# Fused attention and two expert layers on one core: the two halves of a null-key mean on two partitions

## The chip, the cores and the metric

The kernel runs on one core of a Trainium2 chip. The metric is device time in microseconds (us), the median of several runs of the whole program. A core has five engines with instruction streams of their own: PE (TensorE, matrix multiplication), DVE (VectorE), ACT (ScalarE), POOL (GpSimd) and SP (SyncE, which here only issues DMAs). "PEld" is PE's loading of the stationary operand, which the profile lists apart from the matmuls. "SPq" and "ACTq" are the instructions by which SP and ACT issue DMAs.

## The reference

Three layers run one after the other. The part that the change touches is the first, an attention in which a query sees only the keys that fall into the same hash bucket:

```
q_bucket, k_bucket = 6 sign bits of q @ proj and of k @ proj, as a number
mask   = q_bucket[:, None] == k_bucket[None, :]
scores = where(mask, q @ k.T / 8, -1e9)
attn   = softmax(scores)
x      = attn @ v            # 2 batches, 8 heads, 768 tokens, 64 columns
x      = gated rational layer: g(x @ w_in) @ w_out         # 512 -> 2048 -> 512
out    = top-1 of 8 experts: gate * relu(x @ w1[e]) @ w2[e]  # 512 -> 1024 -> 512
```

A query whose bucket holds no key gets -1e9 everywhere, so its softmax is uniform and its result is the mean of all rows of v. That is the "null-key" term.

## The kernel before, in words

The attention works in 24 units: 2 batches, 3 thirds of the queries (256 each), 4 pairs of heads. For each unit `prep` turns q and k around on PE, splits them into a high and a low float16 part and computes the bucket bits (`ee`, `eq`). `stack_a` and `stack_b` let SP copy these pieces by DMA into operands of 128 partitions (`qa`, `qb`, `kp`). `pass1` (matmul L638, maximum L644) finds the largest score of each query. `pass2` computes the scores again (L718, L719), takes the exponential on ACT (L723 for the first batch, L728 and L729 for the second) and sums the weighted rows of v (L687) into one PSUM tile `av` of 4 blocks of 128 queries, 65 columns each: 64 of v and one of ones, which collects the sum of the weights. In the first batch these matmuls are float32, in the second float16 in three terms.

The null-key term goes into the same tile. `flags` (L612 on) turns a row of query maxima around on PE (L617, tile `pm`), DVE makes a 0/1 flag of each (`mf`), and SP copies the flags by DMA into one partition of the tile `FL` (partition 0 for even units, 32 for odd ones). `values` computes, once for each pair of heads and batch (8 times in all), the mean of v by a matmul with ones (L416), which ACT scales into `v32`. DVE stores its float16 rounding (L419, L438) and the rounding error (L420, L439) as two slots of the tile `vmr`, whose last column holds 1 in the first slot and 0 in the second. With the last block of keys of a unit, each of the 4 query blocks gets two more matmuls (the loop ahead of L687): stationary operand one row of 128 flags, moving operand one row of `vmr`, 65 columns. One adds the high part, the other the low part.

Beside the attention run the splitting of the second layer's weights (tiles `raw`, `bits`, `win`, `wo`) and, from unit 7 on, that layer itself for the query blocks that are ready (matmuls L783 and L824, activation chain L797 to L810). After the attention come the last block of the second layer and then the expert layer (L1291 to L1396).

The order of the instructions on each engine is settled when the program is built. Unit 0 (`start`) and all that follows the second layer are written out by hand. Between them a scheduler places the instructions by priorities and its own estimate of times. An edit in one place can therefore move instructions elsewhere. On each engine the order is then fixed: an instruction that waits holds up those behind it.

Of the kernel before, what the change touches and what calls it, by code (L numbers as in the profile page):

```python
# [8 lines left out]
F16 = mybir.dt.float16  # L9
# [3 lines left out]
ALU = mybir.AluOpType  # L13
# [4 lines left out]
P = 128  # L18
B, H, S, D = 2, 8, 768, 64
NPAIR = H // 2  # L20
# [31 lines left out]
NV = 34  # L52
# [68 lines left out]
def tile_kernel(  # L121
# [16 lines left out]
    dve, act, pool, pe, sp = nc.vector, nc.scalar, nc.gpsimd, nc.tensor, nc.sync  # L138
# [10 lines left out]
    def ps_hid(i, nm):  # L149
        return ps_h.tile([P, 512], F32, tag=f"h{i % 2}", name=nm)  # L150
# [137 lines left out]
    anchor = {}  # L288

    def ps_misc(nm, dtype=F32):  # L290
        if phase["b"]:
            return ps_sc.tile([P, 512], dtype, tag="sc", name=nm)
        phase["n"] += 1
        if phase["n"] % 3 == 0:
            return ps_h.tile([P, 512], dtype, tag="h1", name=nm)
        return ps_x.tile([P, 512], dtype, tag="x", name=nm)
# [79 lines left out]
    def prep(ap, a1p, u):  # L376
# [29 lines left out]
        progress["ready"] = u  # L406
        yield

    def values(ap, u):
        va, vmr = VAS[u % NPAIR], VMR[u % NPAIR]  # L410
        if units[u][0] == 0:
            yield
            pv = ps_misc(f"pv{u}")
            pv3 = pv[:, : 2 * D].rearrange("p (h c) -> p h c", h=2)
            for j in range(NT):
                pe.matmul(pv3[0:NV], ones32, VFS[u][:, :, j, 0:D], start=(j == 0), stop=(j == NT - 1))  # L416
            v32 = ap.tile([NV, 2, D], F32, tag="v32", name=f"v32{u}", bufs=1)
            act.activation(v32, pv3[0:NV], AF.Copy, scale=1.0 / S)
            dve.tensor_copy(vmr[:, 0, :, 0:D], v32)  # L419
            dve.tensor_tensor(vmr[:, 1, :, 0:D], v32, vmr[:, 0, :, 0:D], op=ALU.subtract)  # L420
            yield
            return
        vr = raws["v", u]
        pool.memset(va[:, :, :, D : D + 1], 1.0)
        if u in VAC:
            act.copy(va[:, :, :, 0:D], vr)
        else:
            dve.tensor_copy(va[:, :, :, 0:D], vr)
        (dve if u in VLD else pool).tensor_tensor(va[:, :, :, D + 1 :], vr, va[:, :, :, 0:D], op=ALU.subtract)
        yield  # L430
        pv = ps_misc(f"pv{u}")
        pv3 = pv[:, : 2 * (2 * D + 1)].rearrange("p (h c) -> p h c", h=2)
        for j in range(NT):
            pe.matmul(pv3, ones16, va[:, :, j, :], start=(j == 0), stop=(j == NT - 1))
        v32 = ap.tile([NV, 2, D], F32, tag="v32", name=f"v32{u}", bufs=1)
        act.activation(v32, pv3[0:NV, :, D + 1 :], AF.Copy, scale=1.0 / S)
        dve.scalar_tensor_tensor(v32, pv3[0:NV, :, 0:D], 1.0 / S, v32, op0=ALU.mult, op1=ALU.add)
        dve.tensor_copy(vmr[:, 0, :, 0:D], v32)  # L438
        dve.tensor_tensor(vmr[:, 1, :, 0:D], v32, vmr[:, 0, :, 0:D], op=ALU.subtract)  # L439
        yield  # L440

    def clear_k(eng, t):
# [171 lines left out]
    def flags(ap, u, m16, c0, c1, both=True):  # L614
        n, cs = c1 - c0, slice(c0 * P, c1 * P)
        pm = ps_misc(f"pm{u}_{c0}", F16)
        pe.transpose(pm[0:n, :P], m16[:, :n], ident16)  # L617
        mf = ap.tile([NC, 2, P], F16, tag="mf", name=f"mf{u}_{c0}", bufs=1)
        if both:
            dve.tensor_copy(mf[0:n, 0, :], pm[0:n, :P])  # L620
        dve.tensor_single_scalar(out=mf[0:n, 1, :], in_=pm[0:n, :P], scalar=-MFLOOR, op=ALU.is_ge)
        if both:
            row = QBS[u % 2][96:97, 1, :, :].rearrange("p h q -> p (h q)")
            sp.dma_start(row[:, cs], mf[0:n, 0, :])
        f0 = 32 * (u % 2)
        anchor["fl"] = sp.dma_start(FL[f0 : f0 + 1, cs], mf[0:n, 1, :])


    def pass1(ap, u):
# [26 lines left out]
    def pass2(ap, u, later):  # L656
        b, th, hp = units[u]
        qb = QBS[u % 2]
        va, vmr = VAS[hp], VMR[hp]
        f0 = 32 * (u % 2)  # L660
        st = {}

        def weigh(hhs, j, eh, el):
            if "av" not in st:
                if phase["b"] == 0 and u % 2 == 1:
                    st["av"] = ps_hid(0, f"av{u}")
                else:
                    st["av"] = ps_av.tile([P, 512], F32, tag="av", name=f"av{u}")
            av3 = st["av"][:, : NC * (D + 1)].rearrange("p (c d) -> p c d", c=NC)
            for n in range(len(hhs) * TH):  # L670
                hh, c = hhs[n // TH], hhs[0] * TH + n
                ts_ = slice(n * P, (n + 1) * P)
                if el is None:
                    mms = [((0, D + 1), eh[:, ts_], VFS[hp][:, hh, j, :])]
                else:
                    mms = [
                        ((0, D + 1), eh[:, ts_], va[:, hh, j, 0 : D + 1]),
                        ((0, D), eh[:, ts_], va[:, hh, j, D + 1 :]),
                        ((0, D + 1), el[:, ts_], va[:, hh, j, 0 : D + 1]),
                    ]  # L680
                if j == NT - 1:
                    for i in range(2):
                        lr = FL[f0 : f0 + 1, c * P : (c + 1) * P], vmr[f0 : f0 + 1, i, hh, :]
                        mms.insert(0, ((0, D + 1), *lr))
                for i, (o, l, r) in enumerate(mms):
                    first = "first" not in st
                    m = pe.matmul(  # L687
                        av3[:, c, o[0] : o[1]], l, r,
                        start=first, stop=(j == NT - 1 and i == len(mms) - 1), skip_group_check=True,
                    )  # L690
                    if first:
                        st["first"] = m
                    elif j == 0:
                        order_after(m, st["first"])
            if j == NT - 1 and hhs[-1] == 1:
                with tc.high_priority(offset=FOFF):
                    finish(av3)
# [303 lines left out]
    with ExitStack() as actx:  # L1001
        ap = actx.enter_context(tc.tile_pool(name="ap", bufs=2, side="right"))
        a1p = actx.enter_context(tc.tile_pool(name="a1p", bufs=1, side="right"))
# [19 lines left out]
            t.rearrange("p h t c -> p (h t c)").bitcast(F16)[:, :NVA].rearrange("p (h t c) -> p h t c", h=2, t=NT)  # L1023
            for t in VFS
        ]
        VMR = [a1p.tile([NV, 2, 2, D + 1], F16, name=f"vmr{i}") for i in range(NPAIR)]
        FL = a1p.tile([NV, NC * P], F16, name="FL")
        clear_k(dve, KPS[0])
        clear_q(dve, 0)
        for t in VMR:  # L1030
            pool.memset(t[:, 0, :, D : D + 1], 1.0)
            pool.memset(t[:, 1, :, D : D + 1], 0.0)

        def weights():
            ahead = list(wq)
# [21 lines left out]
        for u in range(NU):  # L1057
            assert u == 0 or progress["s1"] >= u * N1, u
            for st, _ in enumerate(pass2(ap, u, later) if u else p2, 0 if u else 1):
# [27 lines left out]
                n = min(goal - progress["s1"], N1P) if u > 0 else N1 - progress["s1"] - (NT - 1 - st) if progress["ready"] else 0  # L1087
# [185 lines left out]
    halves = [s for s in range(NEARLY, NMAIN) if half(s)]  # L1273
# [245 lines left out]
    with tc.manual_schedule(engines=EALL):  # L1519
# [26 lines left out]
        for t in range(TH):  # L1546
# [15 lines left out]
            op=ALU.mult,  # L1562
# [26 lines left out]
            op=ALU.is_equal,  # L1589
# [7 lines left out]
            op=ALU.is_equal,  # L1597
# [98 lines left out]
```

## Time and profile before

| | |
|---|---|
| median of 3 runs | 806.24 us (805.02 to 807.43) |
| profiled execution | 808.09 us, of which its span is 806.4 us |
| PE busy in the span | 737.3 us, 91% |
| DVE busy | 629.4 us, 78% |
| ACT busy | 552.3 us, 68% |
| POOL busy | 321.8 us, 40% |
| mean granted clock of PE | 0.965 of full |

The span runs from the first to the last instruction of one execution. Busy time is not bound time: an engine that is busy 78% of the span may be what everyone waits for in one stretch and idle in another, so the tables by stretch further down are what counts. The granted clock is the share of PE's full clock that the chip allowed.

### The profile page before, as it was taken

The page shows a single profiled execution, that of the slowest core. Times are in us where ns is not written, and L with a number is a line of the kernel's source. Part 1 is how long each engine was busy: PE and PEld are TensorE (multiplying, and loading weights), DVE is VectorE, ACT ScalarE, POOL GpSimd, SP SyncE. Part 2 cuts the span into 40 slices and gives each one's busy share as a digit, 9 for nine tenths or more (in the row PEclk, how much of TensorE's full clock was granted, in tenths as well). Part 3 has the DMA queues.
Part 4 walks back from the last instruction along what each step waited for, and adds up shares of the span by engine and source line. Part 5 has one row for each costly group of instructions (what it writes and reads, how often), then busy time and mean ns, then how long its engine had stood idle before and what let it go on. Part 6 is the DMA issues. An engine that isn't in the chain of part 4 may idle for free. (4 is left out here: it accounts for less than half of the span.)

```text
span 806.4 us, 19020 instructions
## 1 busy us (share of the span) xinstructions
PE 737.3 (91%) x6951; PEld 523.9 (65%) x6951; DVE 629.4 (78%) x1214; ACT 552.3 (68%) x953; POOL 321.8 (40%) x291
## 2 busy tenths in 40 slices
PE   3869799999999999999999999999578999999995
PEld 1448578877777667776777777667345676666763
DVE  5577888789996787768666856776877898989981
ACT  2325335557666777787888887884875698988981
POOL 5101120335353555555565564441520374334320
PEclk9789999989999999999999999999699999999998
DMA  9556554325542211111111100000601358765950
GB/s 220 118 126 178 151 140 137 99 78 141 141 119 46 75 25 22 28 42 24 28 21 35 22 2 18 11 1 28 235 1 40 100 210 280 255 206 188 350 191 3
DMA packets 76297, 83.36 MB, mean 103 GB/s; under 512 B 38634, under 2 KB 56582, under 8 KB 76200
## 3 DMA queue, kind: packets, MB, share of 16 engines
q1 hardware_dynamic: 43672, 50.88, 21.3%
q10 hardware_dynamic: 30064, 24.27, 10.9%
q0 software_dynamic: 2464, 6.95, 2.4%
q8 instruction: 56, 0.92, 0.5%
q14 instruction: 41, 0.34, 0.1%
HBM read 113.92 MB, written 6.95 MB: 150 GB/s over the span
## 5 line engine op out<-in xcount | busy, mean ns | idle before, releaser
L687 PE MATMUL av<-vf,ehl 128*128 128x65 f32 (+2 forms) x1440 | 136.7, 227 | 0.7 <-ACT ehl L723 0.5
L801 POOL TENSOR_TENSOR w<-w,qq 128x512 f32<-128x512 f32 x48 | 61.4, 1279 | 162.6 <-ACT w L798 151.1
L1346 DVE SCALAR_TENSOR_TENSOR wl<-wr,wh 128x1024 f16<-128x1024 f32 x88 | 104.1, 1231 | 9.1 <-ACT wh L1338 9.1
L644 DVE TENSOR_REDUCE mx<-s 128x1 f32<-128x512 f32 (+1 forms) x138 | 93.8, 684 | 19.7 <-PE s L638 17.8
L783 PEld LDWEIGHTS <-winh 128*128 128x128 f16 x768 | 74.8, 98 | 24.0 <-issue 1.4
L1338 ACT ACTIVATE wh<-wr 128x1024 f16<-128x1024 f32 x88 | 87.6, 1056 | 0.0
L730 POOL TENSOR_TENSOR ehl<-e,ehl 128x512 f16<-128x512 f32 x60 | 69.4, 1160 | 37.6 <-ACT ehl L729 33.5
L824 PE MATMUL px<-woh,gh 128*128 128x512 f16 x192 | 74.6, 388 | 9.1 <-ACT gh L809 9.1
L1366 PE MATMUL ph<-xst,wh 128*128 128x128 f16 (+1 forms) x1088 | 80.9, 212 | 1.7 <-ACT xst L1293 1.7
L687 PEld LDWEIGHTS av<-vf,ehl 128*128 128x128 f32 x576 | 77.0, 197 | 5.5 <-ACT ehl L723 1.0
L1366 PE MATMUL ph<-xst,wl 128*128 128x128 f16 (+1 forms) x544 | 79.8, 212 | 0.0
L1366 PEld LDWEIGHTS <-wh 128*128 128x128 f16 x1088 | 73.9, 98 | 7.8 <-issue 5.0
L1396 POOL DMA_INDIRECT out_dram<-y,sidx x15 | 38.0, 2533 | 97.8 <-ACT y L1395 97.8
L718 PE MATMUL s<-qb,kp 128*128 128x256 f16 x288 | 73.6, 278 | 3.5 <-DVE mx L644 2.6
L824 PE MATMUL px<-woh,gl 128*128 128x512 f16 x192 | 73.2, 388 | 1.7 <-DVE gl L810 1.7
L824 PE MATMUL px<-wol,gh 128*128 128x512 f16 x192 | 74.6, 389 | 0.0
L719 PE MATMUL s<-qb,kp 128*128 128x256 f16 x288 | 71.3, 279 | 0.0
L723 ACT ACTIVATE ehl<-s 128x512 f32<-128x512 f32 (+1 forms) x78 | 42.8, 572 | 34.2 <-PE s L719 32.5
L805 POOL TENSOR_TENSOR w<-w,h 128x512 f32<-128x512 f32 x48 | 64.1, 1335 | 3.7
L638 PE MATMUL s<-kp,qa 128*128 128x512 f16 (+1 forms) x184 | 52.9, 339 | 9.6 <-DMA kp<-ee 5.1
L783 PE MATMUL ph<-xth,winh 128*128 128x256 f16 x384 | 58.9, 274 | 0.5 <-DVE gl L810 0.5
L783 PE MATMUL ph<-xtl,winh 128*128 128x256 f16 x384 | 59.0, 274 | 0.0
(318 smaller groups left out, 1809.1 us busy)
## 6 DMA issues: line engine op xcount, KB each, us to landing
wr<-in_moe_w_dram SPq DMA_DIRECT2D x88, 512.0 KB
woh<-in_moe_w_dram SPq DMA_DIRECT2D x36, 512.0 KB
wol<-in_moe_w_dram SPq DMA_DIRECT2D x36, 512.0 KB
rawi<-in_moe_w_in_dram ACTq DMA_DIRECT2D x16, 512.0 KB
rawo<-in_moe_w_out_dram ACTq DMA_DIRECT2D x16, 512.0 KB
x2d<-x SPq DMA_DIRECT2D x12, 256.0 KB
qb<-hq SPq DMA_DIRECT2D x47, 64.0 KB
kp<-hk SPq DMA_DIRECT2D x15, 192.0 KB
```

The source lines that it names most:

```text
L644: anchor["max"] = dve.reduce_max(flat[:, i : i + len(parts)], ps.rearrange("p (n k) -> p n k", n=len(parts)), axis=AX)
L687: m = pe.matmul(av3[:, c, o[0] : o[1]], l, r, start=first, stop=(j == NT - 1 and i == len(mms) - 1), skip_group_check=True,)
L718: pe.matmul(o, kp[:, 1, ks], qb[:, 0, hh, :], start=True, stop=False)
L719: anchor["s2"] = pe.matmul(o, kp[:, 0, ks], qb[:, 1, hh, :], start=False, stop=True)
L730: (dve if j in ELD else pool).tensor_tensor(el, e32, eh, op=ALU.subtract)
L783: pe.matmul(ph[:, i * QC : (i + 1) * QC], w[:, dc, fs], x[:, dc, :], start=(m == 0 and dc == 0), stop=(m == 2 and dc == NDC - 1),)
L801: pool.tensor_tensor(w, w, qq, op=ALU.mult)
L805: pool.tensor_tensor(w, w, h32, op=ALU.add)
L824: pe.matmul(pxs[t], g[:, ts_], w[:, f, :], start=(f == 0 and n == 0), stop=(f == NFC - 1 and n == 2))
L1338: act.activation(WH[s, c], raw(s, c), AF.Copy, scale=sc_of(c))
L1346: dve.scalar_tensor_tensor(WL[s, c], raw(s, c), sc_of(c), WH[s, c], op0=ALU.mult, op1=ALU.subtract)
L1366: pe.matmul(ph[:, f4, :w], m[s, c][:, fs], x, start=(n == 0), stop=(n == 3 * NDC - 1))
```

## The change

The high and the low half of the mean no longer stand in two slots of one partition but on two neighbouring partitions: high on partition 0 (and 32), low on all others, among them 1 (and 33). The flags are copied twice, to both partitions. One matmul with two rows then adds both halves. A new function `halves` fills the tile: DVE rounds `v32` into a tile `v16` and writes the rounding error to all 34 partitions of `vmr`, then POOL copies the rounded row over it on partitions 0 and 32.

```diff
+    def halves(ap, u, v32):
+        vmr = VMR[u % NPAIR]
+        v16 = ap.tile([NV, 2, D], F16, tag="v16", name=f"v16{u}", bufs=1)
+        dve.tensor_copy(v16, v32)
+        dve.tensor_tensor(vmr[:, :, 0:D], v32, v16, op=ALU.subtract)
+        for r in (0, 32):
+            pool.tensor_copy(vmr[r : r + 1, :, 0:D], v16[r : r + 1])
...
     def values(ap, u):
...
-            dve.tensor_copy(vmr[:, 0, :, 0:D], v32)
-            dve.tensor_tensor(vmr[:, 1, :, 0:D], v32, vmr[:, 0, :, 0:D], op=ALU.subtract)
+            halves(ap, u, v32)
...
     def flags(ap, u, m16, c0, c1, both=True):
...
-        anchor["fl"] = sp.dma_start(FL[f0 : f0 + 1, cs], mf[0:n, 1, :])
+        for r in (f0, f0 + 1):
+            anchor["fl"] = sp.dma_start(FL[r : r + 1, cs], mf[0:n, 1, :])
...
     def pass2(ap, u, later):
...
                 if j == NT - 1:
-                    for i in range(2):
-                        lr = FL[f0 : f0 + 1, c * P : (c + 1) * P], vmr[f0 : f0 + 1, i, hh, :]
-                        mms.insert(0, ((0, D + 1), *lr))
+                    mms.insert(0, ((0, D + 1), FL[f0 : f0 + 2, c * P : (c + 1) * P], vmr[f0 : f0 + 2, hh, :]))
...
-        VMR = [a1p.tile([NV, 2, 2, D + 1], F16, name=f"vmr{i}") for i in range(NPAIR)]
+        VMR = [a1p.tile([NV, 2, D + 1], F16, name=f"vmr{i}") for i in range(NPAIR)]
...
         for t in VMR:
-            pool.memset(t[:, 0, :, D : D + 1], 1.0)
-            pool.memset(t[:, 1, :, D : D + 1], 0.0)
+            pool.memset(t[:, :, D : D + 1], 0.0)
+            for r in (0, 32):
+                pool.memset(t[r : r + 1, :, D : D + 1], 1.0)
```

In the changed file the lines stand a little lower: the weighted sum is L693 (before L687), the flag copy L634 (before L626). The instructions move on the engines too. Three places show it; a number behind an underscore in a name only tells tiles apart.

On PE, at the end of unit 0's first pair of query blocks, stood one load and one matmul for each half, ahead of the block's own matmul with the exponentials (`ehl`):

```order
L389 MATMUL pt_q_505<-ident_80,qraw_306 128x128 x2
L687 LDWEIGHTS FL
L687 MATMUL av_487<-vmr_215,FL 128x65
L687 LDWEIGHTS FL
L687 MATMUL av_487<-vmr_215,FL 128x65
L687 MATMUL av_487<-vf_180,ehl_5_493 128x65
```

Now there is one of each, then the block's own matmul, then the next block:

```order
L389 MATMUL pt_q_514<-ident_80,qraw_310 128x128 x2
L693 LDWEIGHTS FL
L693 MATMUL av_496<-vmr_215,FL 128x65
L693 MATMUL av_496<-vf_180,ehl_5_502 128x65
L693 LDWEIGHTS FL
```

In the whole program the flag matmuls go from 192 to 96. Before, 92 pairs stood side by side and 4 pairs were torn apart by other matmuls; now there are 96 single ones. PE's listing shrinks from 13460 to 13272 rows.

On SP, where unit 0 ends and unit 1's operands are copied, the flag copy of unit 0's first two blocks stood ahead of the copies of unit 1:

```order
L479 DMA qb_200<-hq_316 64x256
L626 DMA FL<-mf_0_361 1x2x128
L464 DMA qa_198<-ee_318 24x2x256
L457 DMA kp_203<-hk_317 64x2x768
L457 DMA kp_204<-hk_317 64x2x768
L451 DMA kp_203<-hk_317 64x768
```

Now two flag copies stand there, and all that follows comes one issue later:

```order
L486 DMA qb_200<-hq_320 64x256
L634 DMA FL<-mf_0_365 1x2x128 x2
L471 DMA qa_198<-ee_322 24x2x256
L464 DMA kp_203<-hk_321 64x2x768
L464 DMA kp_204<-hk_321 64x2x768
L458 DMA kp_203<-hk_321 64x768
```

Further on, in unit 1, SP used to copy unit 2's key bits (`kp<-ee`, twice) right behind `kp<-hk` of 64x2x768; in the changed program the two copies `kp<-hk` of 64x768 and one `qb<-qa` go ahead of `kp<-ee`. On PE the matmul into `pm` of unit 1 (L617) used to stand behind the first maxima matmuls of unit 2 (L638) and now stands ahead of them.

On ACT, at the last block of the second layer, the first activation of the expert layer (`hh`, which reads PE's `ph_0_0`) stood between the two steps of `r_6`, the chain of that block:

```order
L803 ACTIVATE r_6_8364<-ph_6_8336,qeps 128x512
L1376 ACTIVATE hh_8510<-ph_0_0_8512 128x512
L804 ACTIVATE r_6_8364<-r_6_8364 128x512
L809 CAST gh_5_8298<-ph_5_8269 128x512
L1338 ACTIVATE wh_4_8393<-wr_7848 128x1024
```

Now it stands further down, ahead of `gh_6`:

```order
L809 ACTIVATE r_6_8321<-ph_6_8293,qeps 128x512
L810 ACTIVATE r_6_8321<-r_6_8321 128x512
L815 CAST gh_5_8255<-ph_5_8226 128x512
...
L806 ACTIVATE ph_7_8360<-ph_7_8360,coef 128x512
L1383 ACTIVATE hh_8467<-ph_0_0_8469 128x512
L815 CAST gh_6_8322<-ph_6_8293 128x512
```

So seven rows of that block's chain and weights pass ahead of `hh`. DVE's `hlo`, which reads `hh`, moves down with it, behind the first step of `ph_7`. Between these places the scheduler also reordered parts of units 1 to 23 on all engines, most of it in units 1 to 11.

## Rows read from the trace of the kernel before

**Rows 1.** Busy time of each engine by stretch, granted clock, DMA share.

```profile
core 0: us, PE busy (x) PEld busy (x) DVE busy (x) ACT busy (x) POOL busy (x), PEclk, DMA share, GB/s
60.00:100.00 40.00, 35.97 (x265) 27.95 (x264) 33.24 (x71) 18.64 (x42) 6.52 (x7) 0.91 0.60 160
300.00:350.00 50.00, 50.00 (x498) 35.55 (x497) 37.60 (x76) 39.31 (x77) 28.41 (x25) 1.00 0.13 27
550.00:600.00 50.00, 36.51 (x301) 23.37 (x299) 36.14 (x91) 33.70 (x52) 17.57 (x13) 0.86 0.26 95
```

**Rows 2.** All instructions that read `FL`: duration in ns, first and last start.

```profile
engine op xcount: duration ns min/median/max, first and last start us, forms
L687 PEld LDWEIGHTS <-FL x192: 90/91/94, 39.2 to 498.2; 1*128 1x128 f16 x192
L687 PE MATMUL av<-vmr,FL x192: 192/198/200, 39.2 to 498.2; 1*128 1x65 f16 x192
```

**Rows 3.** PE by time (start, duration, engine, line, operation): flag pair and successor.

```profile
159.31 0.23 PE L687 MATMUL av<-vmr,FL 1*128 1x65 f16 x2
159.47 0.44 PE L687 MATMUL av<-vf,ehl 128*128 128x65 f32 x2
```

**Rows 4.** PE in order of time, a torn pair: single flag matmuls.

```profile
260.24 0.20 PE L687 MATMUL av<-vmr,FL 1*128 1x65 f16 x1
260.37 0.44 PE L389 MATMUL pt_q<-ident,qraw 128*128 128x128 f32 x2
```

**Rows 5.** SP's DMA issues in order of time, unit 0 to 1.

```profile
29.73 0.60 SPq L479 DMA_DIRECT2D qb<-hq  x1
30.43 0.68 SPq L626 DMA_DIRECT2D FL<-mf  x1
31.21 0.92 SPq L464 DMA_DIRECT2D qa<-ee  x1
...
34.96 1.97 SPq L458 DMA_DIRECT2D kp<-ee  x2
...
37.80 0.61 SPq L626 DMA_DIRECT2D FL<-mf  x1
39.94 1.17 SPq L463 DMA_DIRECT2D qa<-hq  x2
```

**Rows 6.** PE in order of time, the start of unit 1.

```profile
38.42 0.59 PE L638 MATMUL s<-kp,qa 128*128 128x512 f16 x3 [1.13 <-DMA kp<-ee]
```

**Rows 7.** DVE and POOL by time, around unit 0's mean.

```profile
37.35 0.29 DVE L420 TENSOR_TENSOR vmr<-v,vmr 34x128 f16<-34x128 f32 x1
...
30.62 0.67 POOL L393 TENSOR_TENSOR hk<-t_k,hk 128x256 f16<-128x256 f32 x1 [3.96 <-ACT hk L392]
```

**Rows 8.** The instructions on the tile `vmr`, columns as in rows 2: memsets.

```profile
L1031 POOL MEMSET vmr<- x4: 148/149/150, 4.9 to 5.1; 34x2 f16 x4
```

**Rows 9.** SP and PE in order of time, unit 1 to 2.

```profile
51.04 1.64 SPq L458 DMA_DIRECT2D kp<-ee  x2
52.73 1.17 SPq L451 DMA_DIRECT2D kp<-hk  x2
...
50.29 0.39 PE L638 MATMUL s<-kp,qa 128*128 128x512 f16 x1
54.69 1.01 PE L638 MATMUL s<-kp,qa 128*128 128x512 f16 x3 [4.02 <-DMA kp<-ee]
...
58.90 0.42 PE L719 MATMUL s<-qb,kp 128*128 128x256 f16 x1
```

**Rows 10.** The same view as rows 1, for the stretch of unit 1.

```profile
54.00:64.00 10.00, 7.54 (x34) 4.97 (x35) 7.67 (x16) 3.23 (x7) 0.00 (x0) 0.53 0.36 102
```

**Rows 11.** ACT in order of time, last block of the second layer.

```profile
589.25 0.69 ACT L803 ACTIVATE r<-ph,qeps 128x512 f32<-128x512 f32 x1 [1.07 <-DVE ph L807]
590.74 0.60 ACT L1376 ACTIVATE hh<-ph 128x512 f16<-128x512 f32 x1 [0.81 <-PE ph L1366]
591.24 0.62 ACT L804 ACTIVATE r<-r 128x512 f32<-128x512 f32 x1
```

More of the change, by code (lines that the diff above doesn't have):

```diff
@@ L437, in values @@
         dve.scalar_tensor_tensor(v32, pv3[0:NV, :, 0:D], 1.0 / S, v32, op0=ALU.mult, op1=ALU.add)
-        dve.tensor_copy(vmr[:, 0, :, 0:D], v32)
-        dve.tensor_tensor(vmr[:, 1, :, 0:D], v32, vmr[:, 0, :, 0:D], op=ALU.subtract)
+        halves(ap, u, v32)
         yield
```

## The prediction

> **What bounds the kernel now.** I read the busy times by stretch first, because the shares of the whole span mix stages with different limits. From unit 7 on PE is all but full: in 300 to 350 us it is busy 50.00 of 50 us at full clock, while DVE is busy 37.6 and POOL 28.4 [rows 1]. There a saved PE microsecond should come off the end. Between 60 and 100 us PE is busy 36 of 40 us, so some nine tenths of a saving count. In 550 to 600 us PE is busy only 36.5 of 50 us: it waits for the activation chain of the second layer's last block, and the length of that chain decides. In the first 60 us neither holds: PE waits there for DMAs that SP issues one by one.
>
> Next I read the instructions that the edit halves. The 192 flag loads take 91 ns each and the 192 flag matmuls 198 ns [rows 2]. These durations overlap. What a matmul takes from the path is the time from its start to that of its successor, so I read PE in order of time. A pair of flag matmuls starts at 159.31 and its successor at 159.47: 0.16 us [rows 3]. In a torn pair one flag matmul stands alone, at 260.24, and its successor starts at 260.37: 0.13 us [rows 4]. So nearly all of the cost is that of going to one-row operands and back, which stays. The second matmul of a pair adds 0.03 us.
>
> **The change part by part.**
>
> *PE.* 92 pairs lose 0.03 us each: 2.8 us. In 4 torn pairs a whole single visit of 0.13 us goes: 0.5 us. That is 3.3 us. Taking nine tenths of it, by the busy share of the early units, gives 3.0 us. The lower bound is 2.0 us, if the waits of the first ten units swallow more. That two rows cost as much as one is not shown by any row here. The nearest are one-row loads of 90 to 94 ns, all alike [rows 2], and I take no difference.
>
> The one rule that speaks for more: the Trainium skill, "TensorE: Matmul & The Clock Gate", section "LDWEIGHTS (loading the stationary operand)", says that a load's time follows its columns and not its rows, columns divided by 1.2 in ns, an estimate of 107 ns for 128 columns. By that 96 loads would return 10.3 us and the sum would be near 797 us. The trace has 91 ns for the load but only 0.03 us for load and matmul together where they follow another flag pair, and I go by that.
>
> *SP.* `flags` now issues two copies. The first extra one stands where SP issues without a break: 29.73, 30.43, 31.21 and on to the two copies of key bits from 34.96 [rows 5]. PE's first matmul of unit 1 stands idle 1.13 us for just those bits, until 38.42 [rows 6]. From the flag copy to the next issue it is 0.78 us, so that matmul comes 0.78 us later, and with it the flag matmuls of unit 0 that follow at 39.2 [rows 2]. The second extra copy, behind 37.80, is hidden: SP is done with the first at 38.41 and waits until 39.94 for unit 2's q [rows 5]. The later ones stand between waits of SP's own, and I price them at nothing; without that cover each would cost up to the same 0.78 us. Bounds for the term: 0 to 1.6 us. I take 0.78.
>
> The Trainium skill, "DMA: Bandwidth & Descriptors", section "Issuing engines are not separate DMA queues", calls the time that a sequencer needs to initiate a DMA usually small beside the DMA. By that the term would be nothing and the time 0.8 us less; here 0.78 us is most of the distance from issue to issue, and the row decides.
>
> *Means.* DVE does two steps of the same shapes as before: nothing. POOL gets two copies of one partition for each of 8 means. No such copy is in the trace; the nearest are a small memset of 0.15 us [rows 8] and a 128x256 operation of 0.67 us [rows 7]. For unit 0 DVE ends at 37.64, so both copies end between 37.9 and 39.0, ahead of the first flag load at 39.2 [rows 2]. That load comes 0.78 us later still. Behind the copies on POOL stand low halves of k and q and of the second layer's weights, and in the second batch those of the exponentials. If all 16 copies cost 0.67 us and POOL were the limit, it would be 10.7 us; with POOL busy 28.4 of 50 us in the densest stretch [rows 1] I take nothing. Four more memsets in the first microseconds: nothing, since POOL is not what ends there; at most 4 times 0.15 us.
>
> *Moved: `hh` on ACT.* In the last block of the second layer `r_6`'s first step ends at 589.94 (589.25 and 0.69). Its second starts only at 591.24, because `hh` stands between them and waits for PE until 590.74 [rows 11]. With `hh` further down the second step can start 1.30 us earlier. `hh` then costs its 0.50 us (590.74 to 591.24) ahead of `gh_6`. Net 0.8 us off a chain for which PE waits. Bounds 0 to 1.3.
>
> *Moved: units 1 and 2.* Unit 2's key bits, issued at 51.04, now come behind two copies of 1.17 us together and a third of 0.6 to 0.9 us like its neighbours [rows 5, 9]. PE waited 4.02 us for them, until 54.69 [rows 9], and would wait up to 2 us longer. Against it, unit 1's `pm` no longer waits for those bits, so the flags and maxima leave sooner and L719 could start ahead of 58.90. The gap between the first maxima matmuls and 58.90 is 3.2 us, of which some 2 could go, since three maxima matmuls remain to be done. I take zero, between bounds of 2 us either way. The other moves in units 3 to 11 I take as zero as well.
>
> **Sum.** Minus 3.0, plus 0.78, minus 0.8: 3.0 us less. The profiled execution took 808.09 us, a span of 806.4 and 1.7 around it; it becomes 805.1. It stood 1.85 us above the median of 806.24, from which I take the same 3.0 us: **803.2 us**. With the bounds above and the spread of the runs (1.2 us each way) this case alone reaches from 801 to 806.
>
> **Rivals.**
>
> *The saved PE time is taken up by waits.* DVE is busy 33 of 40 us in the early stretch [rows 1], and a PE that comes sooner may only wait longer for its maxima. Then SP's 0.78 and the 0.8 at `hh` are left, and the time is 806.2. Against it stand the stretches with PE at 50.00 of 50.
>
> *A low-clock stretch becomes shorter.* From 54 to 64 us the clock is granted at 0.53, close to the lower level, behind the long wait for unit 2's bits [rows 10]. That costs 4.7 us of PE clock. If `pm`'s new place fills that wait and half of the stretch goes, 2.4 us more are gained: 800.8.
>
> *Every load removed counts in full*, as by the page above. From the row of 91 ns it is 96 times 0.091, 8.7 us, nine tenths of it 7.9: 798.3. The rows of single flag matmuls speak plainly against it.
>
> *Slower: unit 2's bits come too late.* The wait until 54.69 grows by 2.0 us, and PE then stays at the lower level for 10 us more, which costs 5.0. With the sum above that is 4.0 us more than before: 810.2. It decides from a further 7 us at the lower level on. For it speaks that this is the longest wait of PE in the attention; against it that `pm` and unit 1's scores can now run ahead.
>
> **How the numbers follow.** The forecast gets 0.50, the saving taken up by waits 0.24, the shorter low-clock stretch 0.12, loads in full 0.06, the slower case 0.08. What a measurement of this kernel can tell from no change is about 0.3%, 2.4 us, that is from 803.8 to 808.7. Of the forecast's own range some six tenths lie below 803.8. So faster is 0.31 and 0.12 and 0.06, 0.49; within is 0.19 and 0.24, 0.43; slower is 0.08. The range from 799.5 to 808.3 leaves out the loads in full and the slower case.
>
> **What would show it.** Right: 96 flag matmuls, each 0.13 us ahead of its successor; two flag copies on SP at about 30.4 and 31.2 and PE's first L638 of unit 1 near 39.2; `r_6`'s second step directly behind its first; PE still full from 300 to 350 us, and that stage about 3 us ahead. Wrong: a lone two-row matmul that takes 0.16 us; idle time of PE for DVE's maxima that has grown by what was saved; POOL's copies followed by waits of PE for `FL` or `vmr`; another low-clock stretch, or one less, between 50 and 200 us, which would be worth more than the edit.

## The result and the profile after

The changed kernel is slower: 816.75 us median (815.22 to 818.73, 4 runs) against 806.84 us for the kernel before on the same chip. The ratio is 1.0118, with a 95% interval from 1.0071 to 1.0165. The forecast was 803.2 us, and its range ended at 808.3. The profiled execution of the changed kernel took 815.22 us, with a span of 813.5 us and a mean granted clock of 0.961. It was the fastest of the four. The ratios here and below leave out one run each of e7 and e11 that lay more than 1.5% above the fastest of its kernel; the medians have them.

The stretches that answer to [rows 1] and [rows 10], in the view of busy times by window. The columns name themselves; the count of instructions stands in brackets:

```profile
core 0: us, PE busy (x) PEld busy (x) DVE busy (x) ACT busy (x) POOL busy (x), PEclk, DMA share, GB/s
60.00:100.00 40.00, 35.68 (x260) 27.83 (x258) 33.65 (x71) 18.68 (x41) 7.84 (x10) 0.94 0.52 145
300.00:350.00 50.00, 50.00 (x494) 36.06 (x492) 37.06 (x77) 39.34 (x77) 30.03 (x30) 1.00 0.10 22
550.00:600.00 50.00, 40.66 (x350) 27.62 (x348) 36.33 (x94) 35.62 (x57) 18.62 (x14) 0.90 0.30 106
54.00:64.00 10.00, 6.05 (x39) 4.50 (x40) 7.57 (x17) 2.91 (x5) 0.91 (x2) 0.66 0.45 131
```

The steady stretch from 300 to 350 us is as full as before. The flag matmuls, which answer to [rows 2], in the view of one tile's instructions (duration in ns, minimum, median and maximum):

```profile
L693 PEld LDWEIGHTS <-FL x96: 90/91/92, 39.1 to 507.3; 2*128 2x128 f16 x96
L693 PE MATMUL av<-vmr,FL x96: 198/199/200, 39.1 to 507.3; 2*128 2x65 f16 x96
```

And one of them in PE's order of time, with its successor, which answers to [rows 3] and [rows 4]:

```profile
314.95 0.20 PE L693 MATMUL av<-vmr,FL 2*128 2x65 f16 x1
315.08 0.27 PE L693 MATMUL av<-vf,ehl 128*128 128x65 f16 x3
```

So there are 96 instead of 192, two rows load as fast as one, and a single one is 0.13 us from its successor. All this came as forecast. The time went elsewhere, and the table of waits says on whom PE waited. Its columns are what waited, the releaser, then us in total, times, and the longest:

```profile
PE pm L624 <- DVE m L617: 5.9, 3, 3.2
PE s L724 <- DVE mx L652: 3.7, 4, 1.2
PE s L646 <- DMA qb<-qa: 2.9, 1, 2.9
PE s L724 <- DVE mf L628: 2.6, 1, 2.6
PE s L646 <- DMA kp<-ee: 2.4, 1, 2.4
PE s L724 <- DVE ee L401: 1.8, 1, 1.8
```

To see where in the program the time is lost I cut both spans at the same places of the program, not at the same microseconds: at the first transpose of the sums (`xt`) of unit 3, and at that of unit 11. A second execution of the kernel before (its run is told below) serves for the comparison, in the view of busy times by window (columns as above):

```profile
0.00:121.15 121.15, 94.67 (x591) 64.55 (x592) 85.93 (x207) 42.64 (x105) 26.80 (x61) 0.85 0.63 153
121.15:278.37 157.22, 153.29 (x1212) 116.33 (x1212) 136.76 (x256) 100.59 (x200) 60.70 (x59) 1.00 0.40 107
```

The changed kernel, cut at the same places:

```profile
0.00:122.12 122.12, 91.55 (x577) 65.36 (x578) 83.79 (x205) 44.06 (x105) 32.13 (x73) 0.89 0.60 152
122.12:286.49 164.37, 157.16 (x1177) 117.89 (x1177) 137.53 (x259) 102.22 (x200) 62.69 (x61) 0.96 0.38 103
```

Up to unit 3 the changed kernel is 1.0 us later. There PE idles 4.1 us more (30.57 against 26.48), and a granted clock that happened to be higher, 0.89 against 0.85, gives most of it back. From unit 3 to unit 11 it loses 7.15 us. PE idles 7.21 us instead of 3.93. It is also busy 3.9 us longer although it has 35 matmuls fewer, since the granted clock is 0.96 instead of 1.00. Behind unit 11 it gains 1.4 us (527.0 against 528.4 us to the end of the span). The sum is the 6.7 us between the two spans. How the loss divides depends on which execution of the kernel before is taken. The first one, cut at the same places:

```profile
0.00:117.75 117.75, 90.07 (x592) 63.07 (x592) 85.42 (x207) 42.49 (x105) 26.68 (x61) 0.90 0.64 158
117.75:277.36 159.61, 156.26 (x1212) 118.71 (x1212) 136.66 (x256) 101.02 (x200) 60.29 (x59) 0.98 0.40 106
```

Against it the changed kernel loses 4.4 us up to unit 3 and 4.8 from there to unit 11. In both comparisons PE idles 3 to 4 us more in each of the two stretches.

What such a wait looks like, at the worst place. First DVE in order of time in the changed kernel:

```profile
232.12 0.42 DVE L244 TENSOR_SCALAR bitso<-rawo 128x512 int32<-128x512 int32 x1
233.52 0.56 DVE L436 CAST vf<-vraw 128x768 f16<-128x768 f32 x1 [0.98 <-DMA vraw<-in_v_dram]
233.99 0.69 DVE L812 SCALAR_TENSOR_TENSOR ph<-ph,r 128x512 f32<-128x512 f32 x1
234.59 1.70 DVE L245 SCALAR_TENSOR_TENSOR bitso<-rawo,bitso 128x512 int32<-128x512 int32 x1
236.22 0.20 DVE L627 COPY mf<-pm 4x128 f16<-4x128 f16 x1
236.35 0.20 DVE L628 TENSOR_SCALAR mf<-pm 4x128 f16<-4x128 f16 x1
```

Then PE there, with its wait in brackets:

```profile
236.61 0.37 PE L724 MATMUL s<-qb,kp 128*128 128x256 f16 x1 [2.57 <-DVE mf L628]
```

The same place in the second execution of the kernel before:

```profile
229.51 0.21 DVE L620 COPY mf<-pm 4x128 f16<-4x128 f16 x1
229.65 0.20 DVE L621 TENSOR_SCALAR mf<-pm 4x128 f16<-4x128 f16 x1
229.78 0.54 DVE L428 CAST vf<-vraw 128x768 f16<-128x768 f32 x1
```

In the old order the two steps on `mf` stand ahead of the cast of the next values. In the new order they stand behind the cast, which waits 0.98 us for its load, and behind a step of a weight split, which takes 1.70 us where most of its like take 0.68. PE waits 2.57 us for `mf`, against 0.36 us before. The granted clock, at its full level before, falls while PE stands idle and is at the lower level, 0.50, when PE resumes. From 234 to 241 us it is 0.58 in the mean:

```profile
234.00:241.00 7.00, 4.43 (x18) 2.53 (x18) 5.88 (x11) 1.47 (x3) 1.59 (x1) 0.58 0.45 137
```

None of these instructions was edited.

### The profile page after: what moved, and what is told of

Same layout as the page of the kernel before. It is cut to its first block, busy times and chain, and to the rows that moved or that the text cites. A ratio compares the mean times of both kernels' runs of the same rounds, so it can differ in the third digit from the quotient of the medians.

```text
span 813.5 us, 18930 instructions
## 1 busy us (share of the span) xinstructions
PE 737.2 (91%) x6855; PEld 524.0 (64%) x6855; DVE 629.3 (77%) x1214; ACT 554.7 (68%) x953; POOL 343.0 (42%) x311
## 5 line engine op out<-in xcount | busy, mean ns | idle before, releaser
L693 PE MATMUL av<-vf,ehl 128*128 128x65 f32 (+2 forms) x1440 | 138.5, 228 | 0.8 <-ACT ehl L729 0.5
L652 DVE TENSOR_REDUCE mx<-s 128x1 f32<-128x512 f32 x138 | 93.5, 684 | 27.5 <-PE s L646 26.0
L1403 POOL DMA_INDIRECT out_dram<-y,sidx x15 | 48.9, 3257 | 85.6 <-ACT y L1402 85.6
L724 PE MATMUL s<-qb,kp 128*128 128x256 f16 x288 | 74.6, 281 | 8.6 <-DVE mx L652 3.7
L693 PEld LDWEIGHTS av<-vf,ehl 128*128 128x128 f32 x576 | 78.0, 198 | 6.8 <-issue 1.9
L725 PE MATMUL s<-qb,kp 128*128 128x256 f16 x288 | 72.3, 284 | 0.1
```

The lines of the kernel that those rows point to most:

```text
L652: anchor["max"] = dve.reduce_max(flat[:, i : i + len(parts)], ps.rearrange("p (n k) -> p n k", n=len(parts)), axis=AX)
L693: m = pe.matmul(av3[:, c, o[0] : o[1]], l, r, start=first, stop=(j == NT - 1 and i == len(mms) - 1), skip_group_check=True,)
L724: pe.matmul(o, kp[:, 1, ks], qb[:, 0, hh, :], start=True, stop=False)
L725: anchor["s2"] = pe.matmul(o, kp[:, 0, ks], qb[:, 1, hh, :], start=False, stop=True)
```

## The experiments

At first there were two theories. *A:* the loss is the new order of units 1 to 11. *B:* the new operations themselves delay operands, the POOL copies at the head of POOL's queue or the added flag issues on SP. A later form of B for SP alone, the issues and the order they bring, is called *C*. Ratios are to the kernel before on the same chip, with 95% intervals.

**The first four.** *e1.* The matmuls put back as fillers on a row of zeros:

```diff
+                    mms.insert(0, ((0, D + 1), FL[f0 : f0 + 1, c * P : (c + 1) * P], ZR[f0 : f0 + 1, hh, :]))
```

> The changed kernel as it is (two rows of FL, two rounding copies on POOL, the two-row matmul), and ahead of each two-row matmul one more one-row matmul on flag row f0 with a right-hand row of zeros, so that TensorE has as many flag matmuls as before; it adds nothing to the sum. With the 96 matmuls back, the program's order at the splits on DVE falls back nearly to that of before (190 rows of DVE differ, most of them renamed ones, against 514 for the change). Theory A (the loss is the new order of units 1 to 11): 806 to 809 us, without the waits at 202 and 236. Theory B (the POOL copies or the added DMAs delay operands): those are all there and TensorE's saving is gone, so 817 to 820.

Measured: 811.77 us, ratio 1.0031 (1.0006 to 1.0056). Between the ranges of both theories: most of the loss is gone, not all.

*e2.* The low-half matmul dropped, nothing added:

```diff
-                    for i in range(2):
+                    for i in range(1):
                         lr = FL[f0 : f0 + 1, c * P : (c + 1) * P], vmr[f0 : f0 + 1, i, hh, :]
```

> The kernel before without the one-row matmul on the low half of the mean; nothing is added on DVE, POOL or SP. It leaves out the low half of the null-key term. The 96 matmuls are gone, and the order of DVE moves (330 rows). Theory A (a new order costs): slower than before, 809 to 817 us. Theory B (the copies and DMAs cost): only the 3.0 us of the term for TensorE and the tail's 0.8 remain, 802 to 804.

Measured: 810.40 us, ratio 1.0011 (0.9990 to 1.0032). The bare removal of 96 matmuls gains nothing that can be told. Nothing but the order changed with it, so what it saves on PE is lost with the order, as A expected.

*e3.* The POOL copies left out:

```diff
-        for r in (0, 32):
-            pool.tensor_copy(vmr[r : r + 1, :, 0:D], v16[r : r + 1])
```

> The changed kernel without the two POOL copies per mean, so that the high half of the null-key term is left out; the order on PE, DVE, ACT and SP is that of the changed kernel but for a few rows. Theory A: as the changed kernel, 815 to 818 us. Theory B in the form that the copies, which wait up to 9.8 us at the head of POOL's queue, delay the low parts of the queries and keys behind them: 806 to 811.

Measured: 817.69 us, ratio 1.0132 (1.0077 to 1.0187), the same as the changed kernel, with PE's wait for `mf` in the same place (2.9 us in its table of waits). Leaving the copies out gains nothing that four runs can tell, though in the changed kernel POOL stands 20.3 us in all waiting ahead of them. That form of B falls.

*e4.* One flag transfer, the low row's flags fixed at one:

```diff
-        for r in (f0, f0 + 1):
-            anchor["fl"] = sp.dma_start(FL[r : r + 1, cs], mf[0:n, 1, :])
+        anchor["fl"] = sp.dma_start(FL[f0 : f0 + 1, cs], mf[0:n, 1, :])
```

> The changed kernel with one flag transfer per unit instead of two; row f0+1 of FL is set to one for good at the start, so that the low half of the null-key term is taken in for every query whatever its flag. SP issues 25 transfers fewer than the changed kernel; the order moves against it in 164 rows of DVE. Theory B in the form that SP's issues delay the operands: 803 to 808 us. Theory A: 810 to 818, since the splits on DVE stay ahead of where they stood before.

Measured: 813.96 us, ratio 1.0060 (1.0032 to 1.0089). Half the loss goes with the second issue or with the order it brings; the time lies in A's range and not in B's.

These runs also measure what the edit saves on PE where PE is full. The marks are the first transposes of the sums of units 12 and 13, in PE's order of time. The second execution of the kernel before:

```profile
299.58 0.41 PE L760 MATMUL xt<-ident,xu 128*128 128x128 f32 x2
319.25 0.41 PE L760 MATMUL xt<-ident,xu 128*128 128x128 f32 x2
```

The kernel with fillers:

```profile
305.43 0.41 PE L767 MATMUL xt<-ident,xu 128*128 128x128 f32 x2
325.10 0.41 PE L767 MATMUL xt<-ident,xu 128*128 128x128 f32 x2
```

The changed kernel:

```profile
307.74 0.41 PE L766 MATMUL xt<-ident,xu 128*128 128x128 f32 x2
327.29 0.41 PE L766 MATMUL xt<-ident,xu 128*128 128x128 f32 x2
```

A unit takes 19.67 us, with fillers 19.67, changed 19.55: 0.12 us less, that is 4 pairs by 0.03. Not every unit returns it. From unit 12 to unit 19 the changed kernel gains 0.50 us on the first profile of before, where 7 by 0.12 would be 0.84. Three of the seven steps return 0.02 us or nothing.

**The second issue on SP, and a second execution of the kernel before.** *e5.* The kernel before with the flags sent to an unread second row as well:

```diff
+        for r in (f0, f0 + 1):
+            anchor["fl"] = sp.dma_start(FL[r : r + 1, cs], mf[0:n, 1, :])
```

> The kernel before, whole, with the change's second flag transfer alone: each unit's flags are also sent to row f0+1 of FL, which nothing reads. Theory C (the added issues on SP cost in units 0 to 4, where TensorE waits for SP's copies, by their own 0.6 us each and by the order they give): 810 to 812 us, the loss gathered before 140 us and every later unit as before. Theory A (only the missing matmuls' new order costs): 807.8 to 808.6, the one issue at unit 0 at most.

Measured: 810.25 us, ratio 1.0025 (1.0000 to 1.0050). That is some 2 us, at the edge of what can be told, in C's range and above A's. Unit 1's `pm` now stands on PE ahead of unit 2's first maxima matmuls, as in the changed kernel. PE's waits of `pm` for `m` are 5.6 us, against 1.4 in the run that follows, *e6*, which is the kernel before unchanged:

> The kernel before, unchanged, for a second profiled execution. What is looked for is the granted clock between 100 and 120 us, which was 1.00 in the first profile of before and 0.53 to 0.79 over 105 to 115 us in all five others so far. If the stretch is low here too, the 3.5 us that every other kernel loses there against the first profile of before belong to the execution, not to the kernel; if it is at 1.00, to the kernels. The time should be 804 to 812.

Measured: 808.48 us, one run. Its granted clock in three stretches:

```profile
90.00:100.00 10.00, 8.80 (x48) 5.93 (x49) 8.83 (x19) 4.32 (x10) 0.67 (x1) 0.62 0.46 131
105.00:115.00 10.00, 9.64 (x65) 6.67 (x65) 6.53 (x16) 4.60 (x12) 3.03 (x4) 0.83 0.43 130
160.00:170.00 10.00, 9.22 (x76) 7.46 (x75) 8.65 (x18) 7.44 (x14) 4.27 (x4) 1.00 0.36 96
```

The first execution had 0.83, 1.00 and 0.66 in the same stretches. So the same program has its low stretches now here, now there, and a stretch of low clock in one profile cannot be charged to the kernel. Near 110 us, from the first `xt` of unit 2 to that of unit 3, the changed kernel (15.91 us) and the first four experiments lost 3.4 to 4.0 us against the first profile of before (12.35). The second execution takes 13.43 there. So 1.1 us of that loss can be the execution's own, and 2.3 to 2.9 us remain with the kernels.

*e7.* One transfer for both rows, the whole computation kept: the maxima are rounded twice side by side (that part of the edit is left out here), so that the flags stand on 2n partitions:

```diff
...
-        pe.transpose(pm[0:n, :P], m16[:, :n], ident16)
+        pe.transpose(pm[0 : 2 * n, :P], m16[:, : 2 * n], ident16)
...
-        for r in (f0, f0 + 1):
-            anchor["fl"] = sp.dma_start(FL[r : r + 1, cs], mf[0:n, 1, :])
+        anchor["fl"] = sp.dma_start(FL[f0 : f0 + 2, cs], mf[0 : 2 * n, 1, :])
```

> The changed kernel, whole, with one transfer for both flag rows: the rounded maxima are written twice side by side, the transpose gives the flags on 2n partitions, and one transfer lays them on rows f0 and f0+1. SP issues as much as before. Theory C: 811 to 814 us, as with one transfer and a fixed low row (813.96). Theory A alone: 814 to 818, as the changed kernel.

Measured: 808.84 us, ratio 1.0008 (0.9973 to 1.0043). The loss is gone, more than either theory expected. Against the changed kernel SP has an issue less per unit, and the order is another too.

*e8.* The second transfer issued by POOL:

```diff
+        anchor["fl"] = sp.dma_start(FL[f0 : f0 + 1, cs], mf[0:n, 1, :])
+        pool.dma_start(FL[f0 + 1 : f0 + 2, cs], mf[0:n, 1, :])
```

> The changed kernel, whole, with the second flag transfer issued by POOL instead of SP. SP issues as much as before; POOL's queue holds a transfer more per unit, which waits for the flags there. Theory C: 809 to 814 us. Theory A alone: 814 to 818. If transfers on POOL's queue hold up the low parts of queries and keys behind them, over 818.

Measured: 817.39 us, ratio 1.0114 (1.0081 to 1.0147). The time is outside C's range, but the run does not decide against C. Its profile from unit 3 to unit 11 and from there to the end:

```profile
123.37:281.90 158.53, 153.43 (x1190) 116.12 (x1190) 139.21 (x258) 101.84 (x201) 66.42 (x70) 1.00 0.42 109
281.90:815.00 533.10, 489.17 (x5104) 341.62 (x5102) 409.54 (x751) 408.98 (x648) 232.00 (x189) 0.98 0.27 90
```

With SP relieved, units 3 to 11 take 5.8 us less than in the changed kernel (164.37), and PE's long waits of `pm` for `m` are gone from the table. Behind unit 11 it loses 6.1 us (533.1 against 527.0). Half of that comes after the last output transfer is issued by POOL: from the start of that issue to the end of the span it is 10.6 us, where the other 17 traces have 7.2 to 8.1. So the transfers on POOL's queue bring a loss of their own, whose cause was not looked for.

**Other orders of the same work.** *e9 and e10.* The cast that stood ahead of `mf` moved to ScalarE, in the changed kernel and in the kernel before:

```diff
-VAC = (14,)
+VAC = (12, 14)
```

> The changed kernel, whole, with one operation on another engine: the cast of the thirteenth unit's values (vf from vraw), which in the changed kernel's order stands on DVE ahead of the flags of the unit running and waits there 0.98 us for its load, is done by ScalarE. The order moves in 89 rows of DVE around it and hardly elsewhere. Theory A (waits that the order opens on DVE, and the stretch of low clock beside them): the wait of 2.57 us at 236 us and the low stretch from 234 to 241 go, 811 to 814 us. If the flags' lateness there is made by the other work on DVE, no change: 815 to 818.

Measured: 815.99 us, ratio 1.0109 (1.0079 to 1.0138). Its profile shows the wait for `mf` cut to 1.24 us and full clock around it, and that execution, 811.49 us, was the fastest of its kernel and in A's range. The median hardly moved and lies in the range given for no change. So the worst wait of the profile was not the bulk of the loss, and theory A's expectation was wrong.

> The kernel before, whole, with the same cast on ScalarE; 15 rows of DVE's order move. A control: in before the cast stood behind the flags and TensorE waited 0.35 us there, so both theories expect no change, 807 to 809.

Measured: 807.13 us, ratio 1.0006 (0.9984 to 1.0027). No change, as expected.

*e11.* The same on the kernel with one transfer:

> The changed kernel, whole, with one transfer for both flag rows (as before, 808.84) and the cast on ScalarE. There the cast cost nothing visible on TensorE, whose largest wait after 150 us is 0.90 us at 224 us before 287. Theory A: 806 to 810, by the other waits that the new order opens or closes.

Measured: 804.16 us, ratio 0.9967 (0.9944 to 0.9989). This version beats both kernels and keeps the whole computation.

*e12.* That kernel again, with the weight splits given behind the flags. Only the order differs; each engine runs as many instructions as in e11 (6855 matmuls, 1213 on DVE, 954 on ACT, 311 on POOL):

```diff
-        dve.tensor_single_scalar(out=mf[0 : 2 * n, 1, :], in_=pm[0 : 2 * n, :P], scalar=-MFLOOR, op=ALU.is_ge)
+        anchor["max"] = dve.tensor_single_scalar(out=mf[0 : 2 * n, 1, :], in_=pm[0 : 2 * n, :P], scalar=-MFLOOR, op=ALU.is_ge)
```

> The kernel of the run before this one, with the weight splits given behind the unit's flags instead of behind its last row maximum. Another order again (399 rows of DVE against the one-transfer kernel), nothing else. Theory A: anywhere from 803 to 815, and where it lies shows in the idle time of TensorE in units 1 to 11 and its clock there; a theory that rests on the new operations alone expects the same time as the run before.

Measured: 819.55 us, ratio 1.0143 (1.0114 to 1.0172). The same operations in another order cost 15.4 us more. The faster of the two, cut at units 3 and 11 as above:

```profile
0.00:117.45 117.45, 88.53 (x577) 63.41 (x578) 83.82 (x205) 43.55 (x105) 31.53 (x73) 0.91 0.63 158
117.45:274.69 157.24, 152.86 (x1177) 115.50 (x1177) 136.68 (x258) 101.41 (x201) 60.85 (x61) 0.99 0.40 107
```

And the slower:

```profile
0.00:123.40 123.40, 91.92 (x566) 64.23 (x567) 85.77 (x203) 44.05 (x105) 28.84 (x72) 0.86 0.60 147
123.40:288.14 164.74, 157.97 (x1189) 119.24 (x1189) 138.77 (x259) 102.93 (x202) 63.97 (x62) 0.97 0.40 105
```

The slower order loses 6.0 us up to unit 3 and 7.5 us from there to unit 11. In both stretches PE idles 2 to 3 us more (31.5 against 28.9, and 6.8 against 4.4), and the rest goes with a lower granted clock. Behind unit 11 it loses another 2.8 us. The picture is like that of the changed kernel: more idle time of PE and a lower clock.

**Issue or order?** Two runs keep every operation of the changed kernel and move only the order. *e13.* The weight splits dealt out later:

```diff
-WPH = (3, 6, 6, 5, 4, 4, 4)
+WPH = (3, 5, 5, 5, 5, 5, 4)
```

> The changed kernel, whole, with the same weight splits dealt out as 3, 5, 5, 5, 5, 5, 4 over the first seven units instead of 3, 6, 6, 5, 4, 4, 4: from the second unit on each split stands later on DVE (418 rows differ). Both flag transfers on SP stay. Theory A (the order, splits ahead of the maxima and flags): 805 to 812 us. Theory C (the second issue on SP): 814 to 818.

Measured: 815.06 us, ratio 1.0137 (1.0092 to 1.0181). No gain, in C's range and above A's: that the splits stand too early as such is not the cause.

*e14.* Another offset for the priority of the steps that close a unit:

```diff
-FOFF = 100
+FOFF = 200
```

> The changed kernel, whole, every instruction kept, with another priority for the steps that close a unit (an offset of 200 for 100); 390 rows of DVE's order differ. Theory A: another time than 816.75 by more than 3 us, to either side, told by TensorE's idle time before 280 us. Theory C: 814 to 818.

Measured: 811.58 us, ratio 1.0060 (1.0038 to 1.0082). Half of the loss is gone with both issues on SP, by order alone. The sign that A had named, PE's idle time, does not show it. The two stretches of the profile, whose execution was the slowest of the four (815.09 us):

```profile
0.00:124.72 124.72, 93.50 (x574) 65.35 (x575) 81.63 (x202) 42.91 (x104) 29.00 (x72) 0.88 0.59 143
124.72:285.62 160.90, 153.65 (x1181) 115.91 (x1181) 140.41 (x261) 102.07 (x201) 64.94 (x62) 0.99 0.41 110
```

PE idles 31.2 and 7.3 us there, in the changed kernel 30.6 and 7.2. What is gained goes with a higher clock: 0.968 in the mean of the four runs, 0.958 in the changed kernel.

*e15.* The second issue added to the fastest kernel:

```diff
         anchor["fl"] = sp.dma_start(FL[f0 : f0 + 2, cs], mf[0 : 2 * n, 1, :])
+        sp.dma_start(FL[f0 + 1 : f0 + 2, cs], mf[n : 2 * n, 1, :])
```

> The kernel with one transfer for both flag rows and the cast on ScalarE (804.16 us), whole, and the low row's flags sent a second time by a transfer of their own, so that SP issues as often as in the changed kernel; nothing else is added. The order moves too (310 rows of DVE), and lands near that of the changed kernel (243 rows from it). Theories A and C both expect a loss: C some 2 to 4 us by the issues in units 0 to 4 alone, 806 to 808; A with the changed kernel's order the most of its loss, 811 to 817.

Measured: 813.81 us, ratio 1.0097 (1.0066 to 1.0128). One more issue per unit, of which the kernel before lost 2 us, costs 9.7 us here (between two chips; the ratios differ by 1.3%). Its order is near the changed kernel's, and PE's waits of `pm` for `m` are again 5.9 us. That is in A's range and above C's.

*e16.* The later splits on the kernel before, as a control:

> The kernel before, whole, with the splits dealt out as 3, 5, 5, 5, 5, 5, 4. A control for the run on the changed kernel: 326 rows of DVE's order differ from before. Theory A: another time than before, to either side, by up to 8 us; if it is faster by as much as the changed kernel gains, the schedule of the splits helps whatever the flags do.

Measured: 810.35 us, ratio 1.0047 (1.0026 to 1.0068). Dealing out the same splits in other portions costs the kernel before 4 us.

## Why the prediction was wrong

**The step that failed** is the price of the new order, put at nothing. It is the last sentence on the moved parts: "The other moves in units 3 to 11 I take as zero as well." The listing of the order had shown that the scheduler rearranged much there, and the forecast gave it neither a price nor bounds. The runs show what such a rearrangement is worth: 804 to 820 us for the same operations (e11, e12), 812 to 817 for the changed kernel's own (e14 and the result), 806 to 810 for those of the kernel before (e16). That is several times the 3 us that the edit was about. It shows as waits of PE of 0.5 to 3 us for `m`, `mf`, `mx` and `ee`, and as a lower granted clock. For `mf` the cause is shown above: DVE does it behind other work. For unit 1's `m` it is that `pm` now stands ahead of unit 2's maxima on PE. For `mx` and `ee` it was not followed up. Over the 199 runs compared, a run whose mean granted clock is 0.001 lower is 0.47 us longer (a least-squares fit with one slope and a constant for each kernel, whatever the chip; it leaves 1.3 us of scatter). The mean clock is 0.966 in the kernel before and 0.958 in the changed one. So of the 9.2 us between their means some 3.8 go with the lower clock. 5.4 remain at equal clock, and by the same fit the fastest kernel lies 3.4 us under the kernel before. The clock is itself an outcome of what PE does, so this split describes and does not prove.

The same fit shows something that the medians hide. All nine kernels with two flag transfers lie 4.1 to 6.8 us above the kernel before at equal clock: the changed kernel, e1, e3, e5, e8, e9, e13, e14 and e15. Of the seven with one, six lie between 3.4 under and 2.8 above; the seventh is e12, 6.4 above. Against the kernel before on the same chip alone the groups touch: 3.1 to 6.6 us for e1 to e15 with two transfers, at most 3.0 for the six with one. e14's gain over the changed kernel is all clock (5.2 against 5.4 above). A second step is thus in doubt, "The later ones stand between waits of SP's own, and I price them at nothing": the second transfer goes with 3 us or more in every order tried. That an order alone can cost as much is shown by e12.

**PE, minus 3.0.** The mechanism is right: 0.12 us per full unit, no more, and none when fillers are put in. In units 12 to 19 six tenths of it arrive. The Trainium skill, "TensorE: Matmul & The Clock Gate", section "LDWEIGHTS (loading the stationary operand)", holds that rows do not matter to a load. Here two rows load in 91 ns like one, so the trace agrees. That each removed load returns its time, the rival that the prediction made from this, does not hold here: 0.03 us per load and matmul, as forecast.

**SP, plus 0.78.** The first pair of issues in the trace after:

```profile
30.20 1.32 SPq L634 DMA_DIRECT2D FL<-mf  x2
31.62 0.89 SPq L471 DMA_DIRECT2D qa<-ee  x1
```

From the pair to the next issue it is 1.42 us where it was 0.78 [rows 5], so 0.64 more. That size is right for SP. But PE's first matmul of unit 1, forecast near 39.2, starts at 38.34, no later than before (38.42 [rows 6]); it only waits longer, 2.44 us for 1.13. The term's effect on PE is thus not in this trace. What was missing is that the scheduler also reckons with the issue: `pm` moves ahead of unit 2's maxima, and PE then waits for `m`. In the kernel before the issue with all this costs 2 us (0 to 4), above the upper bound of 1.6 at its middle, and on the fastest kernel 9.7.

**Means, nothing.** Right as far as four runs tell, by the run without the copies (e3). The copies themselves, in the view of the tile's instructions, against the bounds of 0.15 and 0.67 us (most lie inside, the longest is 0.68):

```profile
L416 POOL COPY vmr<-v x16: 283/289/684, 36.3 to 336.5; 1x128 f16<-1x128 f16 x16
```

**`hh`, minus 0.8.** Right in place and nearly in size. ACT in the trace after, in answer to [rows 11]:

```profile
597.27 0.69 ACT L809 ACTIVATE r<-ph,qeps 128x512 f32<-128x512 f32 x1 [0.16 <-DVE ph L813]
597.99 0.63 ACT L810 ACTIVATE r<-r 128x512 f32<-128x512 f32 x1
```

The second step follows the first at once. Against the first profile of before the changed kernel is 8.95 us behind ahead of the block (576.20 and 585.15) and 8.24 behind after it (627.13 and 635.37): 0.7 us gained. Against the second execution it is 0.25. Over all 18 traces the stretch between these two matmuls takes 49.9 us on average where `hh` stands lower (8 traces, 49.0 to 50.6) and 50.6 where it stands between the steps (10 traces, 49.6 to 51.2).

**Units 1 and 2, zero.** Within its bounds at that place. PE in the trace after, in answer to [rows 6] and [rows 9]:

```profile
38.34 0.59 PE L646 MATMUL s<-kp,qa 128*128 128x512 f16 x3 [2.44 <-DMA kp<-ee]
55.05 0.26 PE L624 MATMUL pm<-ident,m 128*4 128x128 f16 x1 [3.16 <-DVE m L617]
58.22 1.44 PE L646 MATMUL s<-kp,qa 128*128 128x512 f16 x4 [2.90 <-DMA qb<-qa]
```

The wait for unit 2's bits has become one of `pm` for `m`, with a second one behind it, and the four maxima matmuls start at 58.22, 0.6 us later than in the first profile of before (57.66).

**The rivals.** The saving taken up by waits came true in part of the units. The slower rival had the right sign and the right means, a wait that grows and a clock that stays low, but the wrong place, and one place instead of many. It was given 0.08.

**What stays open.** Which of the moves in units 1 to 11 costs how much was not separated. Taking away the worst wait of the profile did not do it (e9), nor did later splits (e13). How much of the second issue's price is SP's time and how much the order it brings could not be told either: no run had the issue without another order. The one run that took it off SP without dropping it (e8) brought a loss of its own.

## What to carry to other kernels

Where a scheduler sets the order when the program is built, an edit is two changes: the operations, and a new order of everything near them. Price the second by measuring some neutral reorderings of the kernel; here they span several times the edit. Judge the edit itself at an order as near to the old one as can be had, for instance with fillers of the same cost, and then look for a good order with the edit in place, as the version with one transfer and the cast on ScalarE shows: 0.33% faster than before (0.11 to 0.56).

## What the runs showed of the hardware

The granted clock differs from execution to execution of the same program. The 80 runs of the kernel before on four chips range from 804.13 to 813.97 us; the 25 on one of them range from 804.13 to 812.07 us, at mean clocks of 0.961 to 0.971. The low stretches of two profiled ones lie at different places. One profile of each kernel is too little to say where a few microseconds went.

The weight-split step that took 1.70 us on DVE ran while POOL had this instruction under way:

```profile
234.16 1.59 POOL L437 TENSOR_TENSOR vf<-vraw,vf 128x768 f16<-128x768 f32 x1 [4.67 <-DVE vf L436]
```

POOL's ends at 235.75, and DVE's ends 0.54 us later, a little less than its usual 0.68. It is not the only one. In the first profiles of before and after, 64 steps of this line (L245) were run: 14 took over 1 us. Each of the 14 started while POOL had a TENSOR_TENSOR under way and ended 0.54 to 0.56 us after it. The other 50 took 0.65 to 0.69. The kernel before has 8 of the 14 and the changed one 6, so the collisions of this line do not make the loss. The Trainium skill, "SBUF — State Buffer", section "SBUF: two separate sides", says that a DVE operation with two SBUF inputs and a POOL operation that reads SBUF share a pair of ports, and that the later one is blocked until the earlier is done. The traces agree in all 14 cases; no run tested it apart.
